# Laying w_down unevenly over the partitions and loading each half by its own DMA

## The chip, the cores and the metric

The kernel runs on one core of one Trainium2 chip. The metric is the device time in microseconds of one execution. It is quoted as the median over the runs of a kernel.

The DMA engines are the hardware that moves bytes between HBM (the chip's main memory) and SBUF (the core's on-chip memory of 128 partitions). The core has sixteen of them: the profile gives the DMA share over 16 engines. One DMA instruction is cut into packets, each a contiguous run of bytes for one partition: the six loads of 896 KB in the kernel before show as 768 packets of 7168 B, 128 for each load. The packets are dealt out to the engines; a large load shows sixteen increments of its semaphore, as told below.

## The reference

One decode step: a layer norm, attention of 8 batch rows over a window of 1024 cached keys, and a gated feed-forward network (FFN) whose SiLU multiplies the attention's output.

```python
xn = _layernorm(x, axis=-1)                 # x: 8 x 1 x 512, bfloat16
s = _A_ref(xn, A_k_cache, A_v_cache, A_wq, A_wo)       # 32 query heads, 8 kv heads, Dh 128
g = _silu((_gelu(xn @ B_w_gate) * (xn @ B_w_up)) @ B_w_down)   # 512 -> 1792 -> 512
return x + s * g
```

The weights and the window of the caches are 47.5 MB, each byte used once. The part in question, `B_w_down`, is 1792 rows of 512 bfloat16 numbers, 1792 KB of 1024 bytes (1,835,008 bytes), called 1.79 MB below.

## The kernel before

All large loads are issued by SyncE in one order: k_cache and v_cache pieces with wq, then w_gate, w_up, w_down, then wo. They go into a ring of 20 slots. w_down lies with 14 rows on each of 128 partitions and comes in two loads of 7 rows, so one partition gets 7168 contiguous bytes from each load. Cuts are marked `...`; the comments are added.

```python
    FT = F // 4          # 448 columns of the FFN for each of 4 column tiles
    FR = F // P          # 14 rows of w_down on a partition
    ...
    def load_down(h):
        t = slot()
        n = FR // 2 * D
        nc.sync.dma_start(
            out=t[:, 0:n],
            in_=B_w_down.rearrange("(p j) d -> p (j d)", j=FR)[:, h * n : (h + 1) * n],
        )
        return t
    ...
        hT = ffn_sb.tile([P, FR, 32], BF16, name="hT")
        nc.vector.transpose(
            out=hT.rearrange("p j b -> p (j b)"),
            in_=h_sb.rearrange("b (p j) -> b j p", j=FR),
        )
    ...
        for j in range(FR):                      # ffn_down: 28 matmuls
            for t in range(2):
                ...
                nc.tensor.matmul(f_ps[64 * t : 64 * t + 32, 0:256],
                    hT[:, j, :], w[:, c0 : c0 + 256], ...)
```

The softmax here doesn't subtract the row's maximum and nothing guards it: scores larger than these inputs give would overflow.

## Time and profile before

| | before |
|---|---|
| time, median | 123.36 us (4 runs, 122.89 to 123.78) |
| span of the profiled run | 121.3 us |
| bytes read from HBM | 47.46 MB |
| DMA rate from 100 to 112 us | 413 to 423 GB/s |
| last wait for a load of wo ends | 117.15 us |

The page cuts the span in 40 slices. The first line below has the busy share of the sixteen DMA engines in tenths, the second what they moved. The third is the queue of instruction fetches: packets, megabytes, share of time.

```profile
DMA  2999999999999999999999999999999999999820
GB/s 78 394 430 427 427 432 430 416 413 430 424 432 421 430 427 424 408 419 427 432 421 427 419 432 419 421 421 432 430 416 419 419 437 414 416 422 417 343 86 3
...
q8 instruction: 14, 0.23, 0.7%
```

The engines that move data are saturated from the first microseconds to the end: in slices 2 to 37 the share is 0.9 or more, at 394 to 437 GB/s. The kernel is bound by its loads. The end of the chain of waits (start, duration, what) says the same:

```profile
...
82.32 18.72 DMA slot<-in_B_w_up_dram
101.12 16.03 DMA slot<-in_A_wo_dram
117.19 0.64 PE big L469 x8
117.85 0.44 DVE tmp L480
118.37 0.42 DVE out_sb L481
```

The last step of the chain before the final arithmetic is a wait for a load of wo. In the stretches below, PE and PEld are TensorE's matmuls and weight loads, DVE is VectorE, ACT ScalarE and POOL GpSimd; the last three columns are the TensorE clock granted, the DMA share and the rate:

```profile
core 0: us, PE busy (x) PEld busy (x) DVE busy (x) ACT busy (x) POOL busy (x), PEclk, DMA share, GB/s
100.00:104.00 4.00, 1.98 (x20) 0.42 (x15) 2.03 (x4) 1.12 (x2) 0.00 (x0) 0.50 0.99 413
104.00:108.00 4.00, 2.26 (x24) 1.46 (x22) 1.60 (x2) 0.00 (x0) 0.00 (x0) 0.50 1.02 423
108.00:112.00 4.00, 3.12 (x28) 2.03 (x25) 1.40 (x4) 0.75 (x2) 0.00 (x0) 0.50 1.03 423
112.00:116.00 4.00, 2.61 (x32) 2.26 (x32) 0.00 (x0) 0.00 (x0) 0.00 (x0) 0.81 0.77 308
116.00:120.00 4.00, 1.28 (x17) 0.85 (x15) 0.85 (x2) 0.00 (x0) 0.00 (x0) 1.00 0.11 37
```

w_up, w_down and wo pass here at the same 413 to 423 GB/s. In the last two rows the share falls before the loads have ended: some engines are through early. The trace has the time at which each of a load's sixteen parts adds one to the load's semaphore, a counter that the waiting engine reads. The last of the 1 MB loads of wo lands in parts after 0.00 to 0.70 us (eight of them), 1.33 to 1.56 us (three) and 2.84 to 3.01 us (five). In the three 1 MB loads of wo the last part comes after 3.13, 3.11 and 3.01 us; I call these 3.0 to 3.1 us the lead of the early engines. Thirteen instruction fetches of 16 KB, of 0.88 to 0.97 us each, have passed by then (the fourteenth starts at 116.2 us), and 3 x 1 + 5 x 2 = 13: it looks as if eight engines served them all.

The lines of the timeline (start, duration, engine, line, operation, in brackets the idle time before and what ended it) show how the FFN and the last product stand against the loads:

```profile
...
104.88 0.98 DVE L389 STREAM_TRANSPOSE hT<-h_sb 128x448 bf16<-128x448 bf16 x1
...
105.91 3.29 PE L404 MATMUL big<-slot,hT 128*32 128x256 bf16 x28 [1.74 <-DVE hT L389]
...
110.00 1.92 PE L469 MATMUL big<-slot,og 128*64 128x256 bf16 x16 [0.80 <-DMA slot<-in_A_wo_dram]
...
112.47 1.57 PE L469 MATMUL big<-slot,og 128*64 128x256 bf16 x16 [0.55 <-DMA slot<-in_A_wo_dram]
...
117.19 0.63 PE L469 MATMUL big<-slot,og 128*64 128x256 bf16 x8 [0.32 <-DMA slot<-in_A_wo_dram]
```

The transpose of h takes 0.98 us, the 28 matmuls of w_down 3.29 us, and each group of wo's matmuls waits for its load, 0.22 to 0.91 us. So TensorE has slack here.

### The profile page before, as it was taken

The numbers are of one execution on the slowest core, as the hardware profiler recorded it, in microseconds if no ns is written. First come the engines' busy times: TensorE is split into PE (matmuls) and PEld (weight loads), VectorE is DVE, ScalarE is ACT, GpSimd is POOL, SyncE is SP. The second block draws the span as 40 slices with busy tenths as digits, with TensorE's granted clock in tenths as the row PEclk, the third lists the DMA queues.
The fourth block names the chain that finished last, engine by engine and source line by source line (L and its number), as shares of the span: only waits on it lengthen the run. The fifth ranks groups of instructions, "written<-read, shape, count | busy, mean of one in ns | idle before, by whom it ended". The sixth has DMA issues, their size and how long they took to land.

```text
span 121.3 us, 3885 instructions
## 1 busy us (share of the span) xinstructions
PE 96.0 (79%) x1772; PEld 75.6 (62%) x1772; DVE 73.6 (61%) x142; ACT 14.9 (12%) x24; POOL 3.1 (3%) x8
## 2 busy tenths in 40 slices
PE   0197269999999999999799993999999783396660
PEld 0192028897787887887778873897888550064540
DVE  4663035475888887888688882665788644704011
ACT  4000043010101101101101101010101103002000
POOL 7200000000000000000000000000000000000000
PEclk9999955555799999999999999555799955555798
DMA  2999999999999999999999999999999999999820
GB/s 78 394 430 427 427 432 430 416 413 430 424 432 421 430 427 424 408 419 427 432 421 427 419 432 419 421 421 432 430 416 419 419 437 414 416 422 417 343 86 3
DMA packets 7392, 47.72 MB, mean 393 GB/s; under 512 B 808, under 2 KB 976, under 8 KB 2768
## 3 DMA queue, kind: packets, MB, share of 16 engines
q1 hardware_dynamic: 7312, 47.46, 93.6%
q8 instruction: 14, 0.23, 0.7%
q10 hardware_dynamic: 64, 0.02, 0.1%
q14 instruction: 2, 0.02, 0.0%
HBM read 47.46 MB, written 0.01 MB: 391 GB/s over the span
## 4 chain that ended last, share of the span: by engine, by line
DMA 56%; PE 34%; DVE 4%; SPq 2%; issue 1%; DVEq 0%
DMA slot<-in_A_k_cache_dram 17%; DMA slot<-in_B_w_up_dram 15%; PE t_ps L230 15%; DMA slot<-in_A_wo_dram 13%; DMA slot<-in_A_wq_dram 10%; PE sc_ps L253 7%; PE o_ps L282 5%; PE sc_ps L242 3%; DVE kT L234 3%; PE a_ps L273 2%; SPq L84 1%; PE t_ps L345 1%; DVE q_sb L340 1%; SPq L89 1%; PE big L469 1%
## 5 line engine op out<-in xcount | busy, mean ns | idle before, releaser
L234 DVE COPY kT<-t_ps 128x1024 bf16<-128x1024 bf16 x64 | 42.6, 690 | 17.4 <-PE t_ps L230 16.6
L230 PE MATMUL t_ps<-ident,slot 128*128 128x128 bf16 x512 | 43.7, 244 | 2.8 <-DMA slot<-in_A_k_cache_dram 2.8
L230 PEld LDWEIGHTS <-slot 128*128 128x128 bf16 x512 | 35.2, 110 | 3.3 <-DMA slot<-in_A_k_cache_dram 3.0
L253 PEld LDWEIGHTS <-kT 128*128 128x128 bf16 x512 | 18.6, 99 | 9.0 <-DVE kT L234 7.3
L253 PE MATMUL sc_ps<-qT_all,kT 128*128 128x16 bf16 x512 | 22.7, 172 | 1.8
L266 ACT ACTIVATE p<-sc_ps 128x512 bf16<-128x512 f32 x16 | 9.6, 597 | 68.1 <-PE sc_ps L253 68.1
L282 PEld LDWEIGHTS <-slot 128*128 128x128 bf16 x512 | 15.7, 98 | 3.5 <-issue 2.2
L282 PE MATMUL o_ps<-p,slot 128*128 128x16 bf16 x512 | 15.7, 171 | 0.0
L290 DVE TENSOR_REDUCE sums<-a_ps 128x16 f32<-128x512 f32 x16 | 11.1, 692 | 1.4 <-PE a_ps L273 1.0
L469 PE MATMUL big<-slot,og 128*64 128x256 bf16 x64 | 5.8, 332 | 2.8 <-DMA slot<-in_A_wo_dram 2.8
L273 PE MATMUL a_ps<-p,ones_pp 128*128 128x512 bf16 x16 | 7.1, 442 | 0.7 <-ACT p L266 0.7
L242 PE MATMUL sc_ps<-far,hot 4*128 4x512 bf16 x16 | 7.3, 453 | 0.0
L469 PEld LDWEIGHTS <-og 128*64 128x64 bf16 x64 | 4.5, 135 | 4.3 <-issue 2.8
L330 PE MATMUL big<-slot,xT 128*32 128x512 bf16 x32 | 3.4, 516 | 3.9 <-DMA slot<-in_A_wq_dram 3.9
L362 PE MATMUL big<-slot,xT 128*32 128x448 bf16 x32 | 3.6, 566 | 2.0 <-DMA slot<-in_B_w_up_dram 2.0
L294 DVE TENSOR_TENSOR oT_all<-o_ps,sums 128x16 bf16<-128x16 f32 x16 | 3.7, 230 | 1.7
L404 PE MATMUL big<-slot,hT 128*32 128x256 bf16 x28 | 3.3, 415 | 1.7 <-DVE hT L389 1.7
L330 PEld LDWEIGHTS <-xT 128*32 128x32 bf16 x32 | 0.9, 104 | 5.8 <-issue 5.7
L340 DVE CAST q_sb<-big 128x512 bf16<-128x512 f32 x1 | 0.7, 692 | 6.2 <-PE big L330 6.2
L293 DVE RECIPROCAL sums<-sums 128x16 f32<-128x16 f32 x16 | 4.0, 253 | 0.5
L480 DVE TENSOR_TENSOR tmp<-big,g_sb 128x256 f32<-128x256 f32 x1 | 0.4, 425 | 6.2 <-PE big L469 6.2
L404 PEld LDWEIGHTS <-hT 128*32 128x32 bf16 x28 | 2.1, 138 | 3.3 <-DVE hT L389 2.5
(50 smaller groups left out, 28.5 us busy)
## 6 DMA issues: line engine op xcount, KB each, us to landing
slot<-in_A_k_cache_dram SPq DMA_DIRECT2D x16, 1024.0 KB, 19.7
slot<-in_A_v_cache_dram SPq DMA_DIRECT2D x16, 1024.0 KB, 20.3
slot<-in_A_wq_dram SPq DMA_DIRECT2D x4, 1024.0 KB, 9.7
slot<-in_A_wo_dram SPq DMA_DIRECT2D x3, 1024.0 KB, 17.7
slot<-in_B_w_gate_dram SPq DMA_DIRECT2D x2, 896.0 KB, 19.4
slot<-in_B_w_up_dram SPq DMA_DIRECT2D x2, 896.0 KB, 18.6
slot<-in_B_w_down_dram SPq DMA_DIRECT2D x2, 896.0 KB
slot<-in_A_wo_dram SPq DMA_DIRECT2D x1, 512.0 KB
```

The lines of the kernel that those rows point to most:

```text
L230: nc.tensor.transpose(kp[:, c * P : (c + 1) * P], k_t[g][:, r * Dh : (r + 1) * Dh], ident)
L234: nc.vector.tensor_copy(out=kT, in_=kp)
L242: nc.tensor.matmul(sc.rearrange("p r q -> p (r q)"), hot, far.rearrange("n r q -> n (r q)"), start=True, stop=False, skip_group_check=True,)
L253: nc.tensor.matmul(sc[:, r, :], kT_t[g, t][:, c * P : (c + 1) * P], qT_all[:, i, b, :, :].rearrange("p n j -> p (n j)"), start=False, stop ...
L266: nc.scalar.activation(out=p, in_=sc_t[g], func=ACT.Exp, scale=inv_sqrt_dh)
L273: nc.tensor.matmul(sums_ps.rearrange("p r q -> p (r q)"), ones_pp, p.rearrange("p r q -> p (r q)"), start=True, stop=True,)
L282: nc.tensor.matmul(o_ps, v_t[g][:, r * Dh : (r + 1) * Dh], p[:, r, :], start=(r == 0), stop=(r == NKR - 1),)
L290: nc.vector.tensor_reduce(out=sums, in_=sums_ps.rearrange("p r q -> p q r"), axis=AX.X, op=ALU.add)
L293: nc.vector.reciprocal(out=sums, in_=sums)
L330: nc.tensor.matmul(q_ps[i][32 * j : 32 * j + 32, :], xT[:, 0, k, :], wq_t[k][:, n0 : n0 + 512], start=(k == 0), stop=(k == NDC - 1), tile_ ...
L404: nc.tensor.matmul(f_ps[64 * t : 64 * t + 32, 0:256], hT[:, j, :], w[:, c0 : c0 + 256], start=(j == 0), stop=(j == FR - 1), tile_position= ...
L469: nc.tensor.matmul(s_ps[64 * t : 64 * t + 64, 0:256], og[:, hh, j, :], wo_t[q][:, c0 : c0 + 256], start=(n == 0), stop=(n == len(rows) - 1 ...
```

## The change

The intent can be read from the numbers: partitions 0 to 63 are to get 12 rows and 64 to 127 are to get 16, so that whichever engines serve the lower half move fewer bytes. The layout needs four column tiles of 512 instead of 448 (the first three overlap), two transposes, and 32 matmuls, of which 8 use only partitions 64 to 127.

```diff
-    FT = F // 4
-    FR = F // P
+    FT = 512
+    FR0, FR1 = 12, 16
+    F0 = [0, 32 * FR0, 64 * FR0, 64 * FR0 + 32 * FR1]
...
     def load_down(h):
+
         t = slot()
-        n = FR // 2 * D
-        nc.sync.dma_start(
-            out=t[:, 0:n],
-            in_=B_w_down.rearrange("(p j) d -> p (j d)", j=FR)[:, h * n : (h + 1) * n],
-        )
+        for a, z, r0, n in ((0, 64, 0, FR0), (64, P, 64 * FR0, FR1)):
+            m = n // 2 * D
+            nc.sync.dma_start(
+                out=t[a:z, 0:m],
+                in_=B_w_down[r0 : r0 + 64 * n, :].rearrange("(p j) d -> p (j d)", j=n)[
+                    :, h * m : (h + 1) * m
+                ],
+            )
         return t
...
-        hT = ffn_sb.tile([P, FR, 32], BF16, name="hT")
-        nc.vector.transpose(
-            out=hT.rearrange("p j b -> p (j b)"),
-            in_=h_sb.rearrange("b (p j) -> b j p", j=FR),
-        )
+        hT = ffn_sb.tile([P, 2, FR1 // 2, 32], BF16, name="hT")
+        for a, z, n in ((0, 64, FR0), (64, P, FR1)):
+            nc.vector.transpose(
+                out=hT[a:z, :, 0 : n // 2, :],
+                in_=h_sb[a:z, 0 : 32 * n].rearrange("b (p h c) -> b h c p", h=2, c=n // 2),
+            )
...
-        for j in range(FR):
+        rows = [(h, c) for h in range(2) for c in range(FR1 // 2)]
+        for n, (h, c) in enumerate(rows):
+            a = 0 if c < FR0 // 2 else 64
             for t in range(2):
...
-                    hT[:, j, :],
-                    w[:, c0 : c0 + 256],
+                    hT[a:P, h, c, :],
+                    wd_t[h][a:P, c0 : c0 + 256],
```

I call a load of 64 partitions a half-load, and one of 128 partitions a whole load.

More of the change, by code (lines that the diff above doesn't have):

```diff
@@ L364, in ffn_up @@
                         xT[:, 1, k, :],
-                        ws[k // 2][:, (k % 2) * F + j * FT : (k % 2) * F + (j + 1) * FT],
+                        ws[k // 2][:, (k % 2) * F + F0[j] : (k % 2) * F + F0[j] + FT],
                         start=(k == 0),
@@ L399, in ffn_down @@
         f_ps = ps_big.tile([P, 512], FP32, name="big")
-        for j in range(FR):
+        rows = [(h, c) for h in range(2) for c in range(FR1 // 2)]
+        for n, (h, c) in enumerate(rows):
+            a = 0 if c < FR0 // 2 else 64
             for t in range(2):
-                w = wd_t[j // (FR // 2)]
-                c0 = (j % (FR // 2)) * D + t * 256
+                c0 = c * D + t * 256
                 nc.tensor.matmul(
                     f_ps[64 * t : 64 * t + 32, 0:256],
-                    hT[:, j, :],
-                    w[:, c0 : c0 + 256],
-                    start=(j == 0),
-                    stop=(j == FR - 1),
-                    tile_position=(0, 64 * t),
+                    hT[a:P, h, c, :],
+                    wd_t[h][a:P, c0 : c0 + 256],
+                    start=(n == 0),
+                    stop=(n == len(rows) - 1),
+                    tile_position=(a, 64 * t),
                     skip_group_check=True,
```

## The prediction

> **What bounds the kernel now.** The DMA rings. The slices of the page show them 90 to 99% busy from the first to the 37th of 40, at about 425 GB/s. The chain of waits, from 54 us on, is mostly loads: k_cache, w_up, then wo (16.0 us) up to 117.15 us. The tail is uneven: by the stretches of one microsecond the DMA share is 1.01 at 113 us, then 0.63, 0.41, 0.38, 0. The semaphore increments of the last loads say why: each load lands in sixteen parts, eight of them within 0.8 us, three 1.4 to 1.7 us later, five 2.9 to 3.1 us later. Thirteen instruction fetches of 16 KB (0.9 to 1.0 us each) precede that, and 3x1 + 5x2 = 13: eight engines alone pay for them, and the time ends on those eight.
>
> **Intent.** If partitions 0 to 63 are served by those eight engines, 12 instead of 14 rows relieve each by 2 x 64 x 1 KB / 8 = 16 KB, at 8192 B per 0.309 us 0.62 us.
>
> **Why I doubt it.** [...] x_sb's load shows eight packets with eight semaphore writes, and x_res's two loads, to partitions 0-7 and 64-71, hit engines with the same offsets in time. [...] w_down (1.79 MB, 4.3 us at full rate) takes up to twice as long, +4.3 us[...].
>
> **Moved on the engines.** FT 448 to 512 lengthens matmuls and elementwise steps by a seventh: about 0.1 us on each (0.62 and 0.4 us now). The transpose of h (0.98 us) becomes two, an estimated 1.96 us. w_down takes 32 matmuls instead of 28 (3.29 us now): +0.5 us. About +1.7 us before wo's matmuls, which wait for loads 2.8 us in all: hidden. Two more DMA issues (0.33 us each) are hidden too: wo is issued 14 to 18 us before it lands.
>
> **Time.** Rebalanced: about 123.1. Sixteen engines[...]: 123.8. Full conflict: 128. A conflict, whole or partial, is likelier than not: 126.2 us, 8 in 10 between 123.0 and 128.5. Faster by over 2%: 0.03; within: 0.47; slower by over 2%: 0.50.
>
> **What would show it.** A conflict: packets of 6144 and 8192 B of w_down longer than in proportion to 0.309 us, a dip of GB/s to some 200 to 300 in the stretches around 101 to 109 us with the DMA share still near 1, wo landing 1 to 4 us later. No conflict: GB/s flat at 420. Rebalanced: each half-load shows only eight late increments, the tail of DMA share shorter by 0.6 us.
>
> **What would make it wrong.** Engines chosen by partition (a small gain); [...] conflict only among engines that have slack.

The marks show what was cut: reasons and figures that no trace or run of this case shows. "Conflict" there means that half-loads slow each other because of the partitions they write to. 128 us for the full conflict is 123.8, the case of sixteen engines without a conflict, plus 4.3 us for w_down taking at most twice as long, 128.1 in all. The 4.3 us at the full rate follow from 1.79 MB at about 425 GB/s; the factor of two was the author's estimate.

## More of the kernel before

All runs quoted here are undisturbed. The kernel before has two close values, about 122.9 and 123.7 us, and its runs in the different batches mix them.

## The result and the profile after

| | before | after |
|---|---|---|
| time, median of 4 runs | 123.36 us | 129.66 us (129.17 to 130.19) |
| span of the profiled run | 121.3 us | 128.3 us |
| DMA rate from 100 to 112 us | 413 to 423 GB/s | 224 to 235 GB/s |
| last wait for a load of wo ends | 117.15 us | 124.24 us |

The change made the kernel slower: ratio 1.0513, 95% interval 1.0442 to 1.0583. A ratio here is the mean time of one kernel's fast runs over that of the other's of the same rounds, so it is not quite the ratio of the medians quoted.

The same slices after the change:

```profile
DMA  3999999999999999999999999999999999999820
GB/s 84 401 439 416 439 419 432 416 419 434 411 445 409 437 411 432 416 429 419 419 429 419 429 422 434 416 429 419 418 422 428 284 225 230 213 280 418 342 93 3
```

The share of the engines is still full, but from slice 32 to 36 the rate has fallen to half. Busy engines that move half as much are neither idle nor waiting for an issue; each packet takes longer: the 8192 B packets of w_down took 0.576 us in the median, against 0.309 us undisturbed. In stretches of four microseconds (columns as before):

```profile
100.00:104.00 4.00, 1.05 (x9) 0.29 (x8) 2.23 (x4) 1.23 (x2) 0.00 (x0) 0.50 1.02 235
104.00:108.00 4.00, 1.05 (x8) 0.14 (x7) 0.67 (x1) 0.00 (x0) 0.00 (x0) 0.50 1.00 229
108.00:112.00 4.00, 1.90 (x16) 0.98 (x16) 1.96 (x3) 0.00 (x0) 0.00 (x0) 0.50 1.07 224
112.00:116.00 4.00, 0.94 (x12) 0.59 (x12) 0.00 (x0) 0.00 (x0) 0.00 (x0) 0.50 0.99 292
116.00:120.00 4.00, 3.40 (x30) 2.05 (x28) 1.39 (x4) 0.75 (x2) 0.00 (x0) 0.50 1.02 417
```

The page of issues (destination and source, queue, count, size) shows the four half-loads:

```profile
...
slot<-in_B_w_down_dram SPq DMA_DIRECT2D x2, 512.0 KB
slot<-in_B_w_down_dram SPq DMA_DIRECT2D x2, 384.0 KB
```

The chain now waits for w_down, and wo comes 7.1 us later than before:

```profile
...
87.22 20.43 DMA slot<-in_B_w_down_dram
107.73 16.52 DMA slot<-in_A_wo_dram
124.29 0.65 PE big L476 x8
```

The timeline has the longer engine work, and that it is not what the end waits for:

```profile
...
108.06 1.95 DVE L395 STREAM_TRANSPOSE hT<-h_sb 64x384 bf16<-64x384 bf16 x2
...
110.10 2.00 PE L411 MATMUL big<-slot,hT 128*32 128x256 bf16 x16 [2.81 <-DVE hT L395]
...
115.16 2.00 PE L411 MATMUL big<-slot,hT 128*32 128x256 bf16 x16 [3.06 <-DMA slot<-in_B_w_down_dram]
...
117.23 1.92 PE L476 MATMUL big<-slot,og 128*64 128x256 bf16 x16
...
124.29 0.64 PE L476 MATMUL big<-slot,og 128*64 128x256 bf16 x8 [0.31 <-DMA slot<-in_A_wo_dram]
```

The transposes take 1.95 us instead of 0.98, and the matmuls of w_down come in two groups with a wait of 3.06 us for the second load between them. The first group of wo's matmuls no longer waits, but the last group starts 0.05 us after its wait for a load ends, as before.

The trace also records how long each packet took. Undisturbed, a packet of 4096 B takes 0.159 us, 6144 B 0.234, 7168 B 0.272 and 8192 B 0.309, in both kernels (6144 B only in the changed one). I added up what the packets from 90 us on (for the 8192 B ones of w_down, from 95 us) took beyond that, and divided by sixteen engines:

```
packets, after the change              slowed by over 30%   extra us per engine
w_down, half-loads, 6144 B             109 of 128           1.39
w_down, half-loads, 8192 B             128 of 128           2.30
w_gate and w_up, whole loads, 7168 B    57 of 512           0.90
wo, whole loads, 4096 B                219 of 896           2.31
all, with semaphore writes                                  6.95
all, kernel before                                          0.08
```

The sum, 6.95 us, is the growth of the span, 128.3 - 121.3 = 7.0 us. A little over half of it, 3.69 us, lies on the half-loads themselves, and 3.21 us on loads of w_up and wo, which the change did not touch.

### The profile page after: what moved, and what is told of

Same layout as the page of the kernel before. It is cut to its first block, busy times and chain, and to the rows that moved or that the text cites. A ratio compares the mean times of both kernels' runs of the same rounds, so it can differ in the third digit from the quotient of the medians.

```text
span 128.3 us, 3896 instructions
## 1 busy us (share of the span) xinstructions
PE 95.2 (74%) x1776; PEld 73.7 (57%) x1776; DVE 74.7 (58%) x143; ACT 15.0 (12%) x24; POOL 3.1 (2%) x8
## 4 chain that ended last, share of the span: by engine, by line
DMA 55%; PE 35%; DVE 5%; SPq 2%; issue 1%; DVEq 0%
DMA slot<-in_A_k_cache_dram 16%; DMA slot<-in_B_w_down_dram 16%; PE t_ps L235 15%; DMA slot<-in_A_wo_dram 13%; DMA slot<-in_A_wq_dram 10%; PE sc_ps L258 7%; PE o_ps L287 5%; PE sc_ps L247 3%; DVE kT L239 3%; PE a_ps L278 2%; SPq L85 1%; PE t_ps L350 1%; DVE q_sb L345 1%; SPq L90 1%; PE big L476 1%
## 5 line engine op out<-in xcount | busy, mean ns | idle before, releaser
L235 PE MATMUL t_ps<-ident,slot 128*128 128x128 bf16 x512 | 42.1, 238 | 3.2 <-DMA slot<-in_A_k_cache_dram 3.2
L235 PEld LDWEIGHTS <-slot 128*128 128x128 bf16 x512 | 33.9, 107 | 3.8 <-DMA slot<-in_A_k_cache_dram 3.5
L287 PEld LDWEIGHTS <-slot 128*128 128x128 bf16 x512 | 15.5, 97 | 3.2 <-issue 0.8
L367 PE MATMUL big<-slot,xT 128*32 128x512 bf16 x32 | 4.2, 617 | 6.0 <-DMA slot<-in_B_w_up_dram 5.2
L411 PE MATMUL big<-slot,hT 128*32 128x256 bf16 (+1 forms) x32 | 4.0, 411 | 5.9 <-DMA slot<-in_B_w_down_dram 3.1
L411 PEld LDWEIGHTS <-hT 128*32 128x32 bf16 (+1 forms) x32 | 1.8, 126 | 8.5 <-DVE hT L395 3.7
L335 PE MATMUL big<-slot,xT 128*32 128x512 bf16 x32 | 3.5, 530 | 3.8 <-DMA slot<-in_A_wq_dram 3.8
L426 DVE TENSOR_SCALAR th<-th 8x256 f32<-8x256 f32 x2 | 0.6, 284 | 8.0 <-ACT th L423 8.0
```

What stands on the lines that cost most here:

```text
L235: nc.tensor.transpose(kp[:, c * P : (c + 1) * P], k_t[g][:, r * Dh : (r + 1) * Dh], ident)
L287: nc.tensor.matmul(o_ps, v_t[g][:, r * Dh : (r + 1) * Dh], p[:, r, :], start=(r == 0), stop=(r == NKR - 1),)
L367: nc.tensor.matmul(ps[32 * j : 32 * j + 32, 0:FT], xT[:, 1, k, :], ws[k // 2][:, (k % 2) * F + F0[j] : (k % 2) * F + F0[j] + FT], start=(k ...
L411: nc.tensor.matmul(f_ps[64 * t : 64 * t + 32, 0:256], hT[a:P, h, c, :], wd_t[h][a:P, c0 : c0 + 256], start=(n == 0), stop=(n == len(rows) ...
```

## The experiments

The theories at the start, in short: T1, the destination: loads into partitions 0 to 63 alone, and likewise into 64 to 127 alone, pass at about half the rate. T2, the source: the row pitch in HBM of 12 and 16 KB is slow. T3, the longer work of TensorE and VectorE. T4, any DMA of 64 partitions is slow. Every experiment below starts from the kernel before, except the second, and ran in three rounds against it; each has four runs. The runs of one batch were on one chip, those of different batches on different chips, so each time is compared with the kernel before in its own batch.

### Splitting without the new layout

```diff
         t = slot()
         n = FR // 2 * D
-        nc.sync.dma_start(out=t[:, 0:n], in_=...[:, h * n : (h + 1) * n])
+        for a, z in ((0, 64), (64, P)):
+            nc.sync.dma_start(out=t[a:z, 0:n], in_=...[a:z, h * n : (h + 1) * n])
```

> The kernel before, w_down still 14 rows on every partition, but each half loaded by two DMAs, one for partitions 0 to 63 and one for 64 to 127 (4 DMAs of 448 KB). T1 [...]: as slow as the change, +5 to +7 us (128.5 to 130.5). T2 (the new row pitch of 12 and 16 KB in HBM is what is slow): same as before, 123.4. T3 (the longer work of the engines): same as before. T4 (any DMA of 64 partitions is slow[...]): +5 to +7 us like T1.

Measured: 129.56 us against 123.20, ratio 1.0513, the same as the change. With the old pitch of 14 KB and the old engine work the whole loss is there. T2 and T3 fall.

### The engine work without the split

In the changed kernel the loads of the kernel before are put back (cut):

```diff
-        for a, z, r0, n in ((0, 64, 0, FR0), (64, P, 64 * FR0, FR1)):
-            ...
+        n = 7 * D
+        nc.sync.dma_start(out=t[:, 0:n], in_=B_w_down.rearrange("(p j) d -> p (j d)", j=14)[...])
...
-                c0 = c * D + t * 256
+                c0 = min(c, 6) * D + t * 256
```

> All the engine work of the change (512 columns, two transposes, 32 matmuls) with the loads of the kernel before; the result is wrong on purpose (w_down lies in the old order and row 7 of a half is read as row 6). T1, T2, T4: within 0.5 us of before, the longer work being hidden behind wo's loads. T3: +2 us or more.

Measured: 123.10 us, ratio 0.9977 (0.9939 to 1.0016). The product is wrong; the comparison with the reference passed it all the same, so that comparison cannot tell here whether w_down is right. The timeline of this run:

```profile
...
104.97 1.95 DVE L392 STREAM_TRANSPOSE hT<-h_sb 64x384 bf16<-64x384 bf16 x2
...
106.97 3.93 PE L408 MATMUL big<-slot,hT 128*32 128x256 bf16 x32 [2.77 <-DVE hT L392]
...
117.18 0.72 PE L473 MATMUL big<-slot,og 128*64 128x256 bf16 x8 [0.27 <-DMA slot<-in_A_wo_dram]
```

The transposes cost 0.97 us more and the matmuls of w_down 3.93 instead of 3.29 us, and yet the last group of wo starts at 117.18 us, where it started before. All the extra engine work is hidden behind the loads, as predicted.

### The same extra bytes into two places

Four extra half-loads of 7168 B a partition, 1.79 MB together, are issued ahead of w_down into spare slots. The two kernels differ in the destination alone: `[0:64]` or `[32:96]`.

```diff
+            for q in range(4):
+                nc.sync.dma_start(
+                    out=slot()[0:64, 0 : 7 * D],      # the other kernel: [32:96, 0 : 7 * D]
+                    in_=...[64 * (q // 2) : 64 * (q // 2) + 64, (q % 2) * 7 * D : (q % 2 + 1) * 7 * D],
+                )
             wd_t = [load_down(0), load_down(1)]
```

> The kernel before with four extra DMAs of 64 partitions x 7168 B (1.79 MB together, as much as w_down) ahead of w_down, into spare buffers, all into partitions 0 to 63. At the full rate 1.79 MB cost 4.3 us. T1 and T4: +9 to +12 us against before (4.3 plus 5 to 7). T2 and T3: +4.3 us.

> The same four extra DMAs from the same addresses in HBM, but into partitions 32 to 95[...]. T1: +4.3 to +5.5 us against before, so 4 to 7 us less than the run into partitions 0 to 63. T4: the same as that run, +9 to +12 us. T2: +4.3 us in both.

Measured: into 0 to 63, 135.52 us (+12.3, ratio 1.0982); into 32 to 95, 127.39 us (+4.2, ratio 1.0325). The stretches of the run into 0 to 63:

```profile
100.00:104.00 4.00, 0.94 (x8) 0.28 (x8) 2.03 (x4) 1.00 (x2) 0.00 (x0) 0.50 1.04 242
104.00:108.00 4.00, 0.94 (x8) 0.13 (x7) 1.09 (x2) 0.00 (x0) 0.00 (x0) 0.50 1.02 210
108.00:112.00 4.00, 0.00 (x0) 0.00 (x0) 0.51 (x1) 0.00 (x0) 0.00 (x0) 0.50 1.06 208
112.00:116.00 4.00, 0.00 (x0) 0.00 (x0) 0.00 (x0) 0.00 (x0) 0.00 (x0) 0.50 0.95 187
```

and of the run into 32 to 95:

```profile
100.00:104.00 4.00, 1.71 (x16) 0.41 (x15) 2.03 (x4) 1.07 (x2) 0.00 (x0) 0.50 1.02 420
104.00:108.00 4.00, 0.17 (x4) 0.00 (x0) 1.60 (x2) 0.00 (x0) 0.00 (x0) 0.50 1.00 421
108.00:112.00 4.00, 1.79 (x16) 1.28 (x18) 0.00 (x0) 0.00 (x0) 0.00 (x0) 0.50 1.01 418
112.00:116.00 4.00, 2.62 (x30) 1.78 (x28) 1.40 (x4) 0.75 (x2) 0.00 (x0) 0.82 1.03 425
```

The same bytes from the same addresses, in DMAs of the same shape, pass at 420 GB/s in one case and at 187 to 242 in the other. 4.2 us is what 1.79 MB cost at the full rate. Summed as above, the packets' extra time is 8.24 us per engine into 0 to 63 and 0.08 into 32 to 95, as little as in the kernel before. So T4 falls and T1 stands: it is the place of the partitions that costs. 32 to 95 takes half of its partitions from each side of 64, 0 to 63 all from one. What in the hardware makes the difference, no run shows.

To see that partitions 0 to 63 are not special, the same into the upper half (`[64:128]`):

> Four extra DMAs of 64 partitions x 7168 B as in the run into partitions 0 to 63, but into 64 to 127[...] as slow as into 0 to 63, +11 to +13 us. If something else about partitions 0 to 63 were slow: +4.3 us as into 32 to 95.

Measured: 136.92 us (+13.8, ratio 1.1087). Either half is slow. That the upper one costs 1.5 us more (its packets' extra time is 9.48 us per engine) was not expected and is not explained; the two were measured on different chips.

### Why more than 4.3 us

The prediction had allowed at most a doubling of w_down's own 4.3 us. Two explanations for more were tried. S: while any engine is on a half-load, the loads of the others are slowed as well, so the loss is w_down's time plus the lead of the early engines. P: the loss goes by the bytes of the half-loads. Early in the kernel, before the first instruction fetch at 22 us, the parts of a whole load land within 0.5 us of each other, so w_down was moved there, whole and split:

```diff
-    NSLOT = 20
+    NSLOT = 19
...
-        t = slot()
+        t = persist.tile([P, FR // 2 * D], BF16, name=f"wd{h}")
...
     k_t[0] = load_kv(A_k_cache, *groups[0])
+    wd_t = [load_down(0), load_down(1)]
     wq_t = [load_wq(k) for k in range(NDC)]
```

> The kernel before with w_down's two whole loads issued right after the first k_cache load, into tiles of their own (the ring has 19 slots instead of 20). The control of the next run. At this time no instruction fetch has come yet, so the sixteen parts of a load land within about 0.4 us of each other. w_down lands about 4.3 us after the load ahead of it; the time is within 1 us of before, the same bytes being moved.

> The same, w_down loaded in halves of 64 partitions. S (every engine runs at half its rate as long as any engine is on a half-load, so the loss is w_down's time plus the lead of the early engines: 4.3 + 3.1 us late in the kernel): here the lead is 0.4 us, so w_down takes 8.6 to 9.2 us and the loss is 4.3 to 4.9 us. P ([...] the loss is fixed by the bytes): w_down takes 10.6 us or more and the loss is 6.3 us, as in the change.

Measured: whole, 123.14 us against 123.13 (ratio 0.9977); split, 126.61 us (+3.5, ratio 1.0288). The stretches, whole and then split:

```profile
6.00:10.00 4.00, 3.67 (x32) 3.40 (x33) 2.75 (x5) 0.00 (x0) 0.00 (x0) 1.00 1.03 427
10.00:14.00 4.00, 1.04 (x8) 0.28 (x8) 0.40 (x1) 0.00 (x0) 0.00 (x0) 1.00 1.01 428
14.00:18.00 4.00, 1.28 (x12) 0.41 (x15) 0.00 (x0) 0.00 (x0) 0.00 (x0) 1.00 1.01 426
```

```profile
6.00:10.00 4.00, 3.43 (x32) 3.26 (x33) 2.60 (x5) 0.00 (x0) 0.00 (x0) 1.00 1.01 221
10.00:14.00 4.00, 0.00 (x0) 0.00 (x0) 0.33 (x1) 0.00 (x0) 0.00 (x0) 0.83 0.99 226
14.00:18.00 4.00, 1.04 (x8) 0.28 (x8) 0.00 (x0) 0.00 (x0) 0.00 (x0) 0.50 1.01 426
```

Split, the rate is at half until 14 us. The load ahead of w_down has landed at 5.94 us (whole) and 6.12 us (split), w_down at 10.40 and 14.31 us: 4.46 and 8.19 us. The packets' extra time sums to 4.0 us per engine. This is less than S asked for (4.3 to 4.9), and far from P (6.3). Where the engines run abreast, the split costs 3.5 us, within the 4.3 us that the prediction allowed; late in the kernel it costs 6.4.

The semaphore also settles who moves a half-load. The increments of the first one here, and of an 8-partition load of x_res in the kernel before, in us from the first of those that come with data:

```
64 partitions: 0.00 0.19 0.20 0.22 0.23 0.24 0.26 0.27 0.28 0.30 0.31 0.32 0.34 0.35 0.56 0.62
 8 partitions: 0.00 0.02 0.03 0.04 0.06 0.07 0.09 0.27   (and a single event 3.6 us earlier, at the issue)
```

Sixteen engines share a half-load, so giving partitions 0 to 63 fewer rows doesn't relieve eight engines alone. That all sixteen get equal shares is not seen here: the packed trace doesn't name the engines.

Splitting only the second half of w_down (`if h else ((0, P),)`):

> The kernel before with only the second half of w_down (896 KB) split by partitions. S: the loss is 2.15 + 3.1 = 5.2 us (about 128.5). P: half of the loss of the full split, +3.2 us (about 126.5).

Measured: 128.23 us (+5.1, ratio 1.0384). Half of the half-load bytes cost four fifths of the loss. P falls, and S has the size. Packets slowed here: 221 of wo's 896, and the extra time on wo alone is 2.0 us per engine.

The packets of the changed kernel show S at work. Half-loads are in flight from 99.70 to 113.69 us. Between 112 and 113 us, by the summed time of their packets, only about five engines are on a half-load and eleven on wo; yet the 36 packets of wo that start then take 2.1 times their undisturbed 0.159 us on average, and not one of them less than 1.9 times. Soon after the last half-load packet has ended they are back: the 68 that start from 114.2 to 115 us take 1.1 times. So the loss follows the time in which any engine is on a half-load: 14.0 us at about half the rate, an estimated 7.0 us. That the lead of the early engines is what stretches this time is argued from the sizes of the three runs; no run changed the lead alone.

### Fewer partitions

The extra loads again, with 16 and with 32 partitions (`[0:16]`, `[0:32]`, the source cut to match):

> The kernel before with four extra DMAs of only 16 partitions x 7168 B (0.46 MB together, 1.1 us at the full rate) ahead of w_down, into partitions 0 to 15[...] If the loss goes by the bytes alone[...]: +4.3 us. If such loads only ever halve the rate: +5.3 us. [...]

> The same with 32 partitions (0 to 31[...]; 0.92 MB, 2.15 us). [...] half the rate for 2.15 + 3.1 us: +5.2 + 2.2 = +7.4 us, GB/s near 220. By the bytes alone: +4.3 us. If the rate falls with the number of partitions [...] (a quarter for 32): 3 x 5.2 + 2.2 = +17.9 us.

Measured: 16 partitions, 130.68 us (+7.8, ratio 1.0590); 32 partitions, 131.69 us (+8.8, ratio 1.0639). With the rate halved, S gave +7.4 us for 32 partitions, which is 1.4 us short, and +5.3 for 16, 2.5 us short. For 16 the record expected more of S: its sum came to +13.6 us, a clear miss. It rested on a quarter of the rate, which was the author's estimate and was not shown; its terms are cut. So did the +4.3 us by the bytes. The stretches of that run show less than half of the 413 to 423 GB/s of the kernel before, but not a quarter:

```profile
100.00:104.00 4.00, 0.94 (x8) 0.28 (x8) 2.03 (x4) 0.96 (x2) 0.00 (x0) 0.50 1.06 194
104.00:108.00 4.00, 0.94 (x8) 0.14 (x7) 0.00 (x0) 0.00 (x0) 0.00 (x0) 0.50 1.05 174
```

So S, with a fixed share of the rate, is not a formula for narrower loads. What was measured, whatever the formula: 0.46 MB, worth 1.1 us, cost 7.8 us when laid on 16 partitions, and with 32 partitions the rate fell to between 129 and 237 GB/s from 101 to 111 us, no better than with 64.

## Why the prediction was wrong

- What bounds the kernel: right. Both profiles have the DMA engines full, and the time moved with the loads alone.
- Sixteen engines for 64 partitions, so no relief: right. The half-load's sixteen increments come spread over 0.62 us with the data, and none at the issue. What is left of the prediction's reason is the pair of loads of x_res, to partitions 0 to 7 and 64 to 71: their eight increments come spread over 0.27 and 0.28 us, in the same steps within 0.01 us.
- The conflict at the destination: right, and shown by the pair of runs into 0 to 63 and 32 to 95. The prediction gave this a little more than even odds and put its single number, 126.2 us, between the outcomes. Sharing the sixteen engines is not what costs: the half-loads into 32 to 95 share sixteen engines as well (each has sixteen increments), and cost no more than their bytes, 4.2 us for 1.79 MB.
- The engine work hidden: right. 0.97 us on the transposes (predicted 0.98) and 0.64 us on the matmuls (predicted 0.5), and no change of the time when they stand alone.
- The step that failed is the size of the conflict: "w_down (1.79 MB, 4.3 us at full rate) takes up to twice as long, +4.3 us". That term covers w_down's packets alone; they lost 3.69 us, less than allowed. Left out were the whole loads in flight beside them: 0.90 us on w_gate and w_up, 2.31 us on wo. The sum is 6.95 us instead of 4.3. The prediction had the numbers for an estimate: the five late engines are 3 us behind, so half-loads are in flight on some engine for 4.3 + 3.1 = 7.4 us of work, and at half rate this costs about that much again. The trace has them in flight for 14.0 us. It had described the lead of the early engines, but capped the loss at w_down's own time.
- For that reason the range ended at 128.5 and the measured 129.66 lay outside. The dip of the rate was foretold for 101 to 109 us at 200 to 300 GB/s; in stretches of one microsecond it was 299 GB/s from 100 to 101 us and then 178 to 252 up to 114 us. wo was to land 1 to 4 us later; its last wait ends 7.1 us later.

What stays open. No run shows why a whole load of another engine is slowed by half-loads that go elsewhere: from 101 to 102 us, packets of w_up and of both half-loads alike take 1.8 to 1.9 times as long as undisturbed. Which partitions the eight late engines serve was not settled either. No run found a way to take bytes off them, and no version beat the kernel before; the two that equal it load w_down whole.

## What to carry to other kernels

When loads bound a kernel, look at which partitions a DMA writes before looking at its bytes. Here splitting w_down's whole loads at partition 64 cost 6.4 us, so keep bulk loads at 128 partitions; and if a load must be 64 wide, try a range that straddles partition 64: here 32 to 95 passed at 420 GB/s, 0 to 63 at 187 to 242. A slow load can cost more than its own extra time where the engines are out of step: here 3.21 of the 6.95 us per engine lay on its neighbours, and the same split cost 3.5 us early in the kernel and 6.4 us late. To check a suspicion of this sort, add the same bytes at two destinations; the difference is what the destination costs in that kernel.
